# Strassen products of one stage: sums by vector adds, or accumulated in PSUM

## The chip, the cores and the metric

The kernel runs on one core of a Trainium2 chip. The metric is the device time of one execution in microseconds (us); less is better. Engine names are those of the profile: PE (TensorE), DVE (VectorE), ACT (ScalarE), POOL (GpSimd), SP (SyncE, which only issues transfers here).

## The reference, cut to what matters

```python
attn_out = _attn_ref(q, k, v, phi)            # 4 x 8 x 576 x 64, over 32 memory rows
x = transposed(attn_out)                      # 2304 tokens x 512
x = (x @ w_a * (x @ w_b)) @ w_out             # first block, d_ff 1536
h = x @ w_in                                  # second block, d_ff 2048
g = h * (1.0 / (1.0 + np.exp(-1.702 * h)))
out = g @ w_out2
```

The change touches only `h = x @ w_in` and the gate `g`. The second block's input, its last product and all before it stay as they are.

## The kernel before, in words

**Numbers in two parts.** Float32 products are made from two reduced-precision parts of each operand, hi and lo: hi·hi, lo·hi and hi·lo are added up (`PASSES`). `hi_lo` (line 308) makes them: ACT copies hi out, and then DVE or POOL subtracts hi from the source to get lo (`combine`, the instruction at line 305). The weights come as doubles and are decoded on the chip (lines 424 to 439).

**The stage.** `h = x @ w_in` is done in 24 groups (g, p): g counts eight strips of 256 hidden units, p three thirds of the tokens (2 x 384). A group is a 2 x 2 block product, made from seven products instead of eight, as Strassen and Winograd do. `PRODUCTS` pairs an operand of the weights (A11, A12, A22 and four combinations S1 to S4, all in the slot `win[g]`) with one of the tokens (B11, B21, B22, T1 to T4, in `yc[p]`). A product is six matmuls 128x384 (line 1142: two rows by three passes) into one PSUM bank of the eight in `bank_m`; what has to be summed across products is done behind them. The order of a group is P1, P6, P7, P5, P3, P4, P2 (`quad`).

**The sums.** `kept` (line 1177) copies P1 to SBUF on ACT. `added` (line 1184) makes every other sum on DVE: a PSUM bank plus an earlier sum in SBUF, into a fresh slot of `hb_s`. There are seven such adds a group, by the table `SUMS`. Four of the sums are results: c11, c12, c21, c22. `gate` (line 1194) passes each through the gated function on ACT, and SP's queue stores it to the DRAM buffer `g2d` (line 1196), from which the last product reads it back.

**What sets the order.** The program is emitted once, at build time, by a planner (`Order`). Streams with priorities ask for an engine, a time and perhaps a slot; the planner keeps a clock per engine and emits next what starts first by its own cost figures. On the chip each engine then runs its list strictly in that order and waits on semaphores. `main` (priority 50) issues the PE work. Sums, copies and gates are spawned at priority 0, and the operands' splits and combinations have streams of their own: `combine_weights` fills `win[g]` once a slot is free, and `combine_tokens` fills `yc[p]`.

**The order of groups.** (0, 0) runs alone, ahead of the last eight products of the first block (`proj`, line 864). The rest follows in the order (1,0), (0,1), (1,1), (0,2), (1,2), then three p for each of g = 2 to 5, then (6,0), (6,1), (7,0), (7,1), (6,2), (7,2). `win_s` has two slots; the one of g is released by the last product of its third group, here P2. So the slot of g = 0 goes to g = 2 when (0, 2) ends, one group before (2, 0) needs it. After the stage come the last products (lines 1343 and 1374).

```python
if name == "P2" and p == NP - 1:
    win_s.release(win[g], t)
if name == "P1":
    od.spawn(0, kept(t, q, ps, "s"))
for other, out_, place in SUMS[name]:
    od.spawn(0, added(t, q, ps, other, out_, place, left))
```

Of the kernel before, what the change touches and what calls it, by code (L numbers as in the profile page):

```python
# [11 lines left out]
AF = mybir.ActivationFunctionType  # L12
ALU = mybir.AluOpType
# [6 lines left out]
PE, ACT, DVE, POOL = "PE", "ACT", "DVE", "POOL"  # L20
# [26 lines left out]
class Lengths:  # L47
    dve, act, psum = 68, 94, 52
# [128 lines left out]
def tile_mem_attention_moe_moe2(  # L177
# [13 lines left out]
    nc = tc.nc  # L191
# [7 lines left out]
    P = 128  # L199
# [16 lines left out]
    NG2 = F2 // (G2 * P)  # L216
    N2 = 384
    NP = NT // (2 * N2)
# [8 lines left out]
    od = Order()  # L227
# [9 lines left out]
    g2d = dram.tile([F2, NT], F32, name="g2d")  # L237
# [3 lines left out]
    bank_m, bank_a = Slots(banks[:2]), Slots(banks[2:])  # L241
# [11 lines left out]
    attn_m = [p1.tile([P, 2 * NHG * HT], F32R, name=f"attn{i}") for i in range(2)]  # L253
# [472 lines left out]
    py, pz, pv, bdw, g1_t, g1_all, eff_y, big = None, None, None, [], {}, [], [], {}  # L726

    def give(slots_, views):
        slots_.free += [[x, now()] for x in views]

    def now():
        return od.clock[PE]
# [199 lines left out]
    win_s, hb_s, f_s, fw_s, sb_s, tb_s = Slots(), Slots(), Slots(), Slots(), Slots(), Slots()  # L932
    wo2_t, blocks = {}, []

    def views(m, n, count, o=0):
        return [m[:, o + i * n:o + (i + 1) * n] for i in range(count)]

    YN, WN = N2, 4 * P
    CN, FN, SN, BN = 2 * DM, K4 * NB, 2 * K4 * P, DM
# [9 lines left out]
    def spare():  # L949
        return next(x for x in (whl_a, big["whl_b"]) if x is not wt["o1", NG1 - 1][0])  # L950
# [69 lines left out]
    def room_chunks(*flat):  # L1020
        for x in flat:
            od.mark(now(), "room", "o2", len(wo2))
            wo2.append(x.rearrange("p (i f) -> p i f", i=2))

    def room_split(*flat):
        give(sb_s, [x.rearrange("p (i c t) -> p i c t", i=2, c=K4) for x in flat])
# [101 lines left out]

    sums = {}

    def step(q, name):
        g, p = q
        a, b = PRODUCTS[name]
        t = yield "mark", "win", g, a
        for r in range(2):
            t = max(t, (yield "mark", "yc", p, r, b))
        t, ps = yield PE, t, 1040, bank_m
        w, y = win[g][0][a], yc[p][b]
        n = 0
        for r in range(2):  # L1140
            for (sw, mv) in PASSES:
                nc.tensor.matmul(ps[0][:, :N2], w[:, sw, r, :], y[mv][r], start=(n == 0), stop=(n == 5))  # L1142
                n += 1
        if name == "P2" and p == NP - 1:
            win_s.release(win[g], t)
        if name == "P1":
            od.spawn(0, kept(t, q, ps, "s"))
        left = [len(SUMS[name])]
        for other, out_, place in SUMS[name]:
            od.spawn(0, added(t, q, ps, other, out_, place, left))  # L1150

    SUMS = {
# [3 lines left out]
    }  # L1156
    USES = {"s": 2, "u2": 2, "u3": 2, "u4": 1}

    def get(q, name):
        t = yield "mark", name, q  # L1160
        return t, sums[q, name][0]

    def drop(q, name, t):
        x = sums[q, name]
        x[1] -= 1
        if x[1] == 0:
            hb_s.release(x[0], t)

    def put(t, q, name, s, place):
        sums[q, name] = [s, USES.get(name, 1)]  # L1170
        od.mark(t, name, q)
        if place:
            yield from gate(t, q, *place, s)

    def kept(t, q, ps, name):
        t, s = yield ACT, t, act(N2, True), hb_s
        nc.scalar.activation(out=s[0], in_=ps[0][:, :N2], func=AF.Copy)
        bank_m.release(ps, t)
        yield from put(t, q, name, s, None)

    def added(t, q, ps, other, name, place, left):
        t1, x = yield from get(q, other)
        t, s = yield DVE, max(t, t1), dve(N2), hb_s
        nc.vector.tensor_tensor(out=s[0], in0=ps[0][:, :N2], in1=x[0], op=ALU.add)  # L1184
        left[0] -= 1
        if left[0] == 0:
            bank_m.release(ps, t)
        drop(q, other, t)
        yield from put(t, q, name, s, place)

    def gate(t, q, j, u, c):
        g, p = q
        t, _ = yield ACT, t, act(N2)
        nc.scalar.activation(out=c[0], in_=c[0], func=AF.Gelu_apprx_sigmoid)  # L1194
        k, o = G2 * g + j, (2 * p + u) * N2
        nc.sync.dma_start(out=g2d[k * P:(k + 1) * P, o:o + N2], in_=c[0])
        hb_s.release(c, t + 2500.0)
        od.mark(t, "g2", q, j, u)

# [38 lines left out]
    def split_gated():  # L1238
        for i, o in QUARTERS:
            t = yield "mark", "f", i, o  # L1240
            slot, f = loaded.pop(("f", i, o))
            for s in range(2):
                yield from split_part(t, f[:, :, s * P:(s + 1) * P], "sb", i, o, s)
            for s in range(2):
                t = max(t, (yield "mark", "sb", i, o, s))
            f_s.release(slot, t)
        od.mark(t, "front")
        for i in range(NQ, NW):
            yield from (split_whole(i) if i < NS else sums_gated(i))
# [178 lines left out]
    order = [(0, 0), (1, 0), (0, 1), (1, 1), (0, 2), (1, 2)]  # L1428
# [12 lines left out]
    def main():  # L1441
# [67 lines left out]
        yield from gated(g, 3, 1)  # L1509
        room_gated()  # L1510
        yield from quad(0, 0)
        yield from proj(g, 3, 0)
        yield from proj(g, 3, 1)
# [2 lines left out]
        room_projected()  # L1516
        od.spawn(6, load_gated())
        od.spawn(5, split_gated())
        for q in order[1:]:
            yield from quad(*q)  # L1520
            if q == (NG2 - 1, 0):
                room_chunks(*views(big["wv"], CN, 6), *views(spare(), CN, 2), *views(big["y0"], CN, 2, 14 * WN))
            if q == (NG2 - 1, 1):
                room_split(*views(attn_m[0], SN, 4), *views(attn_m[1], SN, 2))
        od.spawn(9, room_last())
        yield from proj2([(i, s) for i in range(NF) for s in range(2)])
        for i in range(NF, NW):
            yield from (proj2([(i, 0), (i, 1)]) if i < NS else proj2_seven(i))

    def quad(g, p):  # L1530
        for name in ("P1", "P6", "P7", "P5", "P3", "P4", "P2"):
            yield from step((g, p), name)

    with tc.manual_schedule():

# [12 lines left out]
        for n in range(NU):  # L1548
            p = 10 + n if n >= NHG else 10 + PC * n
# [42 lines left out]
```

## Time and profile before

| | us |
|---|---|
| time, median of 3 runs (lowest, highest) | 767.47 (766.93, 768.99) |
| span of the profiled execution | 765.3 |
| PE busy | 752.5 (98%) |
| DVE busy | 613.2 (80%) |
| ACT busy | 386.0 (50%) |
| POOL busy | 359.4 (47%) |

The profile gives the profiled execution its span, from the first instruction to the last, and no other time; the 2.2 us between the span and the median lie outside what the engines show. The table's busy times are means over stages with different limits, so the views that cut the span into stretches say more: they show in which stretch an engine has idle time at all. In rows of the trace, `bank` is a PSUM bank, `wv`, `whl_a`, `attn`, `eff`, `g`, `rest` and `y` are SBUF regions that hold the operands of the stage, `dm` holds decoded weights, and `acc` is a large SBUF region in which the sums and the intermediate tokens lie. A line starts with the time from the start of the span and the duration.

### The profile page before, as it was taken

The page shows a single profiled execution, that of the slowest core. Times are in us where ns is not written, and L with a number is a line of the kernel's source. Part 1 is how long each engine was busy: PE and PEld are TensorE (multiplying, and loading weights), DVE is VectorE, ACT ScalarE, POOL GpSimd, SP SyncE. Part 2 cuts the span into 40 slices and gives each one's busy share as a digit, 9 for nine tenths or more (in the row PEclk, how much of TensorE's full clock was granted, in tenths as well). Part 3 has the DMA queues.
Part 4 walks back from the last instruction along what each step waited for, and adds up shares of the span by engine and source line. Part 5 has one row for each costly group of instructions (what it writes and reads, how often), then busy time and mean ns, then how long its engine had stood idle before and what let it go on. Part 6 is the DMA issues. An engine that isn't in the chain of part 4 may idle for free.

```text
span 765.3 us, 14870 instructions
## 1 busy us (share of the span) xinstructions
PE 752.5 (98%) x5538; PEld 692.7 (91%) x5538; DVE 613.2 (80%) x1086; ACT 386.0 (50%) x854; POOL 359.4 (47%) x335
## 2 busy tenths in 40 slices
PE   8998999999999999999999999999999999999997
PEld 7787788999888979989999999999998888899997
DVE  4888978888877896347999878778796898898884
ACT  4577767454344352225465555454554465444441
POOL 0223442444435342226798655433271059776661
PEclk9999999999999999999999999999999999999999
DMA  8968313232321331000023546454669957544401
GB/s 262 339 213 247 113 38 112 76 108 84 114 79 56 92 113 46 1 1 2 1 69 101 176 149 189 158 179 147 219 241 328 307 179 245 178 139 138 136 23 37
DMA packets 70568, 103.99 MB, mean 136 GB/s; under 512 B 6240, under 2 KB 49248, under 8 KB 70496
## 3 DMA queue, kind: packets, MB, share of 16 engines
q1 hardware_dynamic: 65040, 93.64, 38.4%
q10 hardware_dynamic: 5456, 9.41, 3.5%
q8 instruction: 43, 0.70, 0.4%
q14 instruction: 29, 0.24, 0.1%
HBM read 75.24 MB, written 27.79 MB: 135 GB/s over the span
## 4 chain that ended last, share of the span: by engine, by line
PE 91%; DMA 3%; SPq 2%; DVE 2%; ACT 1%; issue 1%; ACTq 0%; DVEq 0%
PE bank L1142 23%; PE bank L831 19%; PE bank L1374 13%; PE bank L1343 12%; PE bank L887 10%; PE bank L864 10%; PE bank L760 3%; DMA q<-in_q_dram 2%; SPq L320 1%; DMA phi<-in_phi_dram 1%; DMA raw<-in_moe_w_b_dram 1%; SPq L321 1%; PE bank L1436 1%; PE bank L582 1%; SPq L352 0%
## 5 line engine op out<-in xcount | busy, mean ns | idle before, releaser
L305 POOL TENSOR_TENSOR acc<-acc 128x512 f32<-128x512 f32 (+2 forms) x67 | 93.4, 1416 | 75.7 <-ACT attn L311 31.9
L305 DVE TENSOR_TENSOR attn<-acc,attn 128x512 fp32r<-128x512 f32 (+1 forms) x102 | 107.4, 1079 | 13.6 <-ACT attn L311 13.6
L1184 DVE TENSOR_TENSOR acc<-bank,acc 128x384 f32<-128x384 f32 x168 | 89.6, 553 | 30.3 <-PE bank L1142 19.8
L311 ACT ACTIVATE attn<-acc 128x512 fp32r<-128x512 f32 (+2 forms) x117 | 70.6, 611 | 52.5 <-PE bank L1374 31.8
L844 ACT ACTIVATE gr<-bank 128x288 f32<-128x288 f32 x96 | 38.9, 405 | 81.9 <-PE bank L831 67.0
L305 POOL TENSOR_TENSOR y<-gr,y 128x288 fp32r<-128x288 f32 x45 | 38.0, 845 | 78.7 <-ACT y L311 78.5
L1194 ACT ACTIVATE acc<-acc 128x384 f32<-128x384 f32 x96 | 49.1, 522 | 51.0 <-DVE acc L1184 50.0
L847 DVE TENSOR_TENSOR gr<-bank,gr 128x288 f32<-128x288 f32 x96 | 43.4, 454 | 36.2 <-PE bank L831 27.9
L831 PE MATMUL bank<-attn,eff 128*128 128x288 f32 x384 | 54.2, 296 | 0.0
L831 PEld LDWEIGHTS bank<-attn,eff 128*128 128x128 f32 x384 | 51.9, 188 | 1.9 <-ACT plain L424 0.8
L864 PEld LDWEIGHTS bank<-g,whl_b 128*128 128x128 f32 x384 | 51.4, 188 | 1.7 <-ACT g L311 1.7
L864 PE MATMUL bank<-g,whl_b 128*128 128x288 f32 x384 | 52.7, 296 | 0.0
L1142 PE MATMUL bank<-attn,y 128*128 128x384 f32 x288 | 52.3, 335 | 0.0
L907 DVE TENSOR_TENSOR acc<-bank,acc 128x512 f32<-128x512 f32 (+1 forms) x72 | 38.7, 554 | 16.4 <-PE bank L887 15.6
L887 PE MATMUL bank<-y,whl_a 128*128 128x512 f32 (+1 forms) x240 | 51.6, 370 | 0.0
L887 PEld LDWEIGHTS bank<-y,whl_a 128*128 128x128 f32 x240 | 41.4, 188 | 9.8 <-issue 0.8
L1142 PEld LDWEIGHTS bank<-attn,y 128*128 128x128 f32 x288 | 50.1, 188 | 0.0
L305 POOL TENSOR_TENSOR g<-gr,g 128x288 fp32r<-128x288 f32 x28 | 26.1, 937 | 34.9 <-ACT g L311 34.7
L1374 PE MATMUL bank<-y,attn 128*128 128x256 f32 x300 | 41.1, 280 | 0.0
L831 PE MATMUL bank<-attn,eff_b 128*128 128x288 f32 x288 | 40.0, 295 | 0.0
L831 PEld LDWEIGHTS bank<-attn,eff_b 128*128 128x128 f32 x288 | 38.9, 188 | 0.2
L1374 PEld LDWEIGHTS bank<-y,attn 128*128 128x128 f32 x300 | 38.0, 188 | 0.1
(289 smaller groups left out, 1854.9 us busy)
## 6 DMA issues: line engine op xcount, KB each, us to landing
g2d<-acc SPq DMA_DIRECT2D x96, 192.0 KB, 2.1
raw<-in_moe_w_out_dram SPq DMA_DIRECT2D x28, 512.0 KB, 4.4
acc<-g2d SPq DMA_DIRECT2D x10, 1024.0 KB, 6.8
raw<-in_moe_w_in_dram SPq DMA_DIRECT2D x16, 512.0 KB, 3.7
acc<-g2d SPq DMA_DIRECT2D x16, 512.0 KB, 5.8
raw<-in_moe_w_a_dram SPq DMA_DIRECT2D x20, 256.0 KB, 2.8
raw<-in_moe_w_b_dram SPq DMA_DIRECT2D x20, 256.0 KB, 3.1
q<-in_q_dram SPq DMA_DIRECT2D x32, 144.0 KB, 4.4
```

Of the source, the lines that this page charges most:

```text
L305: (nc.gpsimd if e == POOL else nc.vector).tensor_tensor(out=dst, in0=in0, in1=in1, op=op)
L311: nc.scalar.activation(out=hi, in_=src, func=AF.Copy)
L831: nc.tensor.matmul(ps[0][:, :U], e[c][:, sw, i * CW + j * P:i * CW + (j + 1) * P], attn(b, mv, c, u * U, U), start=(n == 0), stop=(n == 3 ...
L844: nc.scalar.activation(out=gr[0], in_=pa_[0][:, :U], func=AF.Copy)
L847: nc.vector.tensor_tensor(out=gr[0], in0=pb[0][:, :U], in1=gr[0], op=ALU.mult)
L864: nc.tensor.matmul(ps[0][:, :U], w[:, sw, j, mb * P:(mb + 1) * P], g1[0][:, j, mv, :], start=(n == 0), stop=(n == 3 * G1 - 1),)
L887: nc.tensor.matmul(ps[0][:, :e - o], w[:, sw, j, mb * P:(mb + 1) * P], g1_all[mv][:, j, o:e], start=(n == 0), stop=(n == 3 * G1 - 1),)
L1142: nc.tensor.matmul(ps[0][:, :N2], w[:, sw, r, :], y[mv][r], start=(n == 0), stop=(n == 5))
L1184: nc.vector.tensor_tensor(out=s[0], in0=ps[0][:, :N2], in1=x[0], op=ALU.add)
L1194: nc.scalar.activation(out=c[0], in_=c[0], func=AF.Gelu_apprx_sigmoid)
L1343: nc.tensor.matmul(ps[i, s][0], b[0][:, sw, c - o, :], wo2[c][:, mv], start=(c == n == 0), stop=(c == 4 * K4 - 1 and n == 2),)
L1374: nc.tensor.matmul(ps[name][0][:, :NB], x[0][:, sw, c, :], moving(b, h // 2 + c, mv), start=(h == c == n == 0), stop=(h > 0 and c == K4 - ...
```

## The change

**Sums in PSUM.** A group's order is now P1, P5, P6, P3, P7, P2, P4. P1, P6, P7 and P4 accumulate into one bank (chain a), P5 and P3 into a second (chain b), and P2 has a third (c). A chained product adds to what is in the bank. Between them ACT takes copies: s after P1, x5 after P5, u2 after P6. DVE makes three adds: c12 = bank b + u2 after P3, c22 = bank a + x5 after P7, c11 = bank c + s after P2, each in place of its SBUF operand. c21 is what stands in bank a after P4, and the gate reads it straight from PSUM (`direct`).

**Waits.** The first matmul of a chained product waits until the sum that stood in the bank has been taken (`AFTER`): P6 for the copy s, P3 for x5, P7 for u2, and P4 for DVE's add c22.

**Two groups alternate.** `quads` sorts the steps of all groups behind (0, 0): step i of the n-th has the key 7n + 2i. So the second half of a group alternates with the first half of the next. (0, 0) stays alone, its steps one behind the other.

**The slot's release** moves with the last step, from P2 to P4.

The matmuls and their operands are the same in number and size: 1008 of line 1142 (now line 1153). DVE's adds go from 168 to 72 (line 1180), ACT's copies from 24 to 72 (line 1172); the 96 gates and 96 stores stay, and 24 of the gates read PSUM.

```diff
+    CHAINS = {"P1": "a", "P6": "a", "P7": "a", "P4": "a", "P5": "b", "P3": "b", "P2": "c"}
+    AFTER = {"P6": "s", "P3": "x5", "P7": "u2", "P4": "c22"}
+    held = {}
...
-        t, ps = yield PE, t, 1040, bank_m
+        chain = CHAINS[name]
+        first = (q, chain) not in held
+        if first:
+            t, held[q, chain] = yield PE, t, 1040, bank_m
+        else:
+            t = max(t, (yield "mark", AFTER[name], q))
+            t, _ = yield PE, t, 1040
+        ps = held[q, chain]
...
-                nc.tensor.matmul(ps[0][:, :N2], w[:, sw, r, :], y[mv][r], start=(n == 0), stop=(n == 5))
+                nc.tensor.matmul(
+                    ps[0][:, :N2], w[:, sw, r, :], y[mv][r], start=(first and n == 0), stop=(n == 5),
+                    skip_group_check=not first,
+                )
...
-        if name == "P2" and p == NP - 1:
+        if name == STEPS[-1] and p == NP - 1:
             win_s.release(win[g], t)
...
+        if name in ("P1", "P5", "P6"):
+            od.spawn(0, kept(t, q, ps, {"P1": "s", "P5": "x5", "P6": "u2"}[name]))
+        elif name == "P4":
+            od.spawn(0, direct(t, q, ps))
+        else:
+            od.spawn(0, added(t, q, ps, *SUMS[name]))
...
+    STEPS = ("P1", "P5", "P6", "P3", "P7", "P2", "P4")
+    SUMS = {"P7": ("x5", "c22", (1, 1)), "P3": ("u2", "c12", (0, 1)), "P2": ("s", "c11", (0, 0))}
...
+    def added(t, q, ps, other, name, place):
+        t = max(t, (yield "mark", other, q))
+        x = sums.pop((q, other))
+        t, _ = yield DVE, t, dve(N2)
+        nc.vector.tensor_tensor(out=x[0], in0=ps[0][:, :N2], in1=x[0], op=ALU.add)
+        od.mark(t, name, q)
+        if name != "c22":
+            bank_m.release(ps, t)
+        yield from gate(t, q, *place, x[0], x, act(N2))
+
+    def direct(t, q, ps):
+        s = yield "slot", hb_s
+        t = yield from gate(max(t, s[1]), q, 1, 0, ps[0][:, :N2], s, act(N2, True))
         bank_m.release(ps, t)
...
+        nc.scalar.activation(out=s[0], in_=src, func=AF.Gelu_apprx_sigmoid)
...
+    def quads(which):
+
+        steps = [(len(STEPS) * n + 2 * i, q, name) for n, q in enumerate(which) for i, name in enumerate(STEPS)]
+        for _, q, name in sorted(steps, key=lambda x: x[0]):
+            yield from step(q, name)
```

**PE, group (0, 0).** Seven products before, by the order P1, P6, P7, P5, P3, P4, P2; `bank_N` are PSUM banks.

```order
-L1142 MATMUL bank_75<-wv,y_1443 128x384 x6
-L1142 MATMUL bank_72<-whl_a,y_1443 128x384 x6
-L1142 MATMUL bank_74<-whl_a,y_1443 128x384 x2
-L1142 MATMUL bank_74<-y_1443 128x384 x4
-L1142 MATMUL bank_73<-wv,y_1443 128x384 x6
-L1142 MATMUL bank_77<-wv,y_1443 128x384 x6
-L1142 MATMUL bank_76<-y_1443 128x384 x6
-L1142 MATMUL bank_78<-wv,y_1443 128x384 x6
```

And with the change, P1, P5, P6, P3, P7, P2, P4:

```order
+L1153 MATMUL bank_75<-wv,y_1443 128x384 x6
+L1153 MATMUL bank_72<-wv,y_1443 128x384 x6
+L1153 MATMUL bank_75<-whl_a,y_1443 128x384 x6
+L1153 MATMUL bank_72<-wv,y_1443 128x384 x6
+L1153 MATMUL bank_75<-whl_a,y_1443 128x384 x2
+L1153 MATMUL bank_75<-y_1443 128x384 x4
+L1153 MATMUL bank_74<-wv,y_1443 128x384 x6
+L1153 MATMUL bank_75<-y_1443 128x384 x6
```

Before, every product has its own bank. Now four of the seven go to bank_75, and the last of them follows the fifth with one product between.

**DVE beside that group, before.** `attn_92<-acc,attn_92` makes lo parts of the tokens' second third, line 426 decodes weights, line 1184 makes the sums.

```order
L305 TENSOR_TENSOR attn_92<-acc,attn_92 128x384 x2
L1184 TENSOR_TENSOR acc<-bank_72,acc 128x384 [waits PE_49,Activation_49,Pool_49]
L426 TENSOR_SCALAR acc<-acc 128x512 [waits Pool_49]
L1184 TENSOR_TENSOR acc<-bank_74,acc 128x384 [waits DVE_49,PE_49]
L1184 TENSOR_TENSOR acc<-bank_73,acc 128x384 [waits PE_49]
L1184 TENSOR_TENSOR acc<-bank_73,acc 128x384 [waits DVE_49]
L1184 TENSOR_TENSOR acc<-bank_77,acc 128x384 [waits DVE_49,PE_49]
L430 TENSOR_SCALAR acc<-acc 128x512
L1184 TENSOR_TENSOR acc<-bank_76,acc 128x384 [waits PE_49]
L434 SCALAR_TENSOR_TENSOR acc<-raw_79,acc 128x512 [waits DMAHW3_49,DVE_49]
L1184 TENSOR_TENSOR acc<-bank_78,acc 128x384 [waits PE_49]
```

With the change:

```order
L305 TENSOR_TENSOR attn_92<-acc,attn_92 128x384 x2
L305 TENSOR_TENSOR acc<-acc 128x384 [waits DVE_49]
L305 TENSOR_TENSOR attn_92<-acc,attn_92 128x384
L426 TENSOR_SCALAR acc<-acc 128x512 [waits Activation_49]
L1180 TENSOR_TENSOR acc<-bank_72,acc 128x384 [waits PE_49,Activation_49]
L305 TENSOR_TENSOR acc<-acc 128x384 [waits DVE_49]
L1180 TENSOR_TENSOR acc<-bank_75,acc 128x384 [waits PE_49]
L1180 TENSOR_TENSOR acc<-bank_74,acc 128x384 [waits PE_49]
```

Before, one sum stood between the lo parts and line 426. Now two more instructions on tokens (`acc<-acc` is a combination, `attn_92` a lo part) stand there, and a third between c12 (bank_72) and c22 (bank_75, for which P4 waits).

**PE where the slot of g = 0 goes to g = 2, with the change.** The first row ends P4 of (0, 2), which releases the slot; bank_75 is P3 of (1, 2), bank_74 is P1 of (2, 0), bank_78 is P7 of (1, 2).

```order
L1153 MATMUL bank_77<-y_1443 128x384
L1153 MATMUL bank_75<-eff_b,y_1443 128x384 [waits Activation_49]
L1153 MATMUL bank_75<-eff_b,y_1443 128x384 x5
L1153 MATMUL bank_74<-wv,y_1443 128x384 [waits Activation_49]
L1153 MATMUL bank_74<-wv,y_1443 128x384 [waits DVE_49]
L1153 MATMUL bank_74<-wv,y_1443 128x384 x4
L1153 MATMUL bank_78<-rest,y_1443 128x384 x6
L1153 MATMUL bank_73<-wv,y_1443 128x384 [waits Activation_49]
```

**DVE at the same place, before.** `y_1443<-dm_84` is the lo part of A11 of g = 2, `y_1443<-dm_85` that of A22.

```order
L1184 TENSOR_TENSOR acc<-bank_72,acc 128x384 [waits PE_49]
L1184 TENSOR_TENSOR acc<-bank_74,acc 128x384 [waits PE_49]
L305 TENSOR_TENSOR y_1443<-dm_84,y_1443 128x256 [waits Activation_49]
L1184 TENSOR_TENSOR acc<-bank_77,acc 128x384 [waits PE_49,Activation_49]
L305 TENSOR_TENSOR y_1443<-dm_85,y_1443 128x256 [waits Activation_49]
```

With the change:

```order
L1180 TENSOR_TENSOR acc<-bank_76,acc 128x384 [waits PE_49]
L1180 TENSOR_TENSOR acc<-bank_75,acc 128x384 [waits PE_49,Activation_49]
L305 TENSOR_TENSOR y_1443<-dm_84,y_1443 128x256 [waits Activation_49]
L305 TENSOR_TENSOR dm_85<-dm_84,dm_85 128x2x128 [waits Pool_49]
L305 TENSOR_TENSOR y_1443<-dm_85,y_1443 128x256 [waits Activation_49]
```

Before, the seven products of (1, 2) stood on PE between the release and P1 of (2, 0); now it is one product. P1 of (2, 0) waits for the lo part, which stands on DVE right behind the add that needs the end of P3 of (1, 2).

## Rows read from the trace of the kernel before

**Rows 1.** Busy time of each engine in five stretches; columns as the head says.

```profile
core 0: us, PE busy (x) PEld busy (x) DVE busy (x) ACT busy (x) POOL busy (x), PEclk, DMA share, GB/s
0.00:105.00 105.00, 96.44 (x1142) 81.00 (x1143) 84.31 (x197) 67.13 (x174) 31.51 (x33) 1.00 0.69 219
105.00:391.00 286.00, 285.95 (x2119) 258.35 (x2118) 222.80 (x422) 131.38 (x306) 125.28 (x126) 1.00 0.20 62
...
404.70:572.40 167.70, 167.70 (x968) 167.70 (x967) 134.97 (x242) 90.03 (x195) 88.77 (x88) 1.00 0.52 174
572.40:761.10 188.70, 188.70 (x1225) 171.97 (x1223) 157.58 (x207) 88.32 (x164) 100.71 (x78) 1.00 0.54 174
761.10:765.30 4.20, 0.00 (x0) 0.00 (x0) 0.42 (x1) 0.00 (x0) 0.00 (x0) 1.00 0.45 120
```

**Rows 2.** The chain that ended last: start us, us, what.

```profile
404.76 167.65 PE bank L1142 x966
```

**Rows 3.** Costliest groups: the page's; then by form, 391 to 573 us.

```profile
L1142 PE MATMUL bank<-attn,y 128*128 128x384 f32 x288 | 52.3, 335 | 0.0
...
L1184 DVE TENSOR_TENSOR acc<-bank,acc 128x384 f32<-128x384 f32 x167 | 89.1, 553 | 30.3 <-PE bank L1142 19.8 <-ACT dm L424 4.8 <-ACT y L311 1.6
...
L1194 ACT ACTIVATE acc<-acc 128x384 f32<-128x384 f32 x92 | 47.4, 523 | 51.0 <-DVE acc L1184 50.0
...
L1177 ACT ACTIVATE acc<-bank 128x384 f32<-128x384 f32 x24 | 11.7, 487 | 5.4 <-PE bank L1142 5.4
```

**Rows 4.** Timeline of PE, 390.9 to 405 us: products 1 and 7.

```profile
390.96 1.21 PE L1142 MATMUL bank<-wv,y 128*128 128x384 f32 x6
...
397.21 1.20 PE L1142 MATMUL bank<-wv,y 128*128 128x384 f32 x6
```

**Rows 5.** Timeline of DVE, 391 to 400 us.

```profile
392.21 2.09 DVE L305 TENSOR_TENSOR attn<-acc,attn 128x384 fp32r<-128x384 f32 x2
394.23 0.55 DVE L1184 TENSOR_TENSOR acc<-bank,acc 128x384 f32<-128x384 f32 x1
394.69 0.77 DVE L426 TENSOR_SCALAR acc<-acc 128x512 f32<-128x512 f32 x1
395.38 1.94 DVE L1184 TENSOR_TENSOR acc<-bank,acc 128x384 f32<-128x384 f32 x4
```

**Rows 6.** DVE's groups by form, 391 to 573 us: two SBUF inputs.

```profile
L305 DVE TENSOR_TENSOR attn<-acc,attn 128x384 fp32r<-128x384 f32 x4 | 4.5, 1132 | 0.0
...
L305 DVE TENSOR_TENSOR acc<-acc 128x384 f32<-128x384 f32 x3 | 3.1, 1021 | 0.0
...
L305 DVE TENSOR_TENSOR g<-acc,whl_b 128x384 fp32r<-128x384 f32 x1 | 0.5, 548 | 0.0
```

**Rows 7.** Timeline of POOL, 392 to 400 us.

```profile
393.85 1.33 POOL L305 TENSOR_TENSOR acc<-acc 128x384 f32<-128x384 f32 x1
395.14 1.19 POOL L305 TENSOR_TENSOR attn<-acc,attn 128x384 fp32r<-128x384 f32 x1
396.30 4.64 POOL L305 TENSOR_TENSOR acc<-acc 128x384 f32<-128x384 f32 x4
```

**Rows 8.** Timeline of ACT, 391 to 394 us: the copy of P1.

```profile
392.68 0.47 ACT L1177 ACTIVATE acc<-bank 128x384 f32<-128x384 f32 x1
```

**Rows 9.** Timelines of PE and of DVE around the hand-over of a weight slot.

```profile
432.71 0.51 PE L1142 MATMUL bank<-eff_b,y 128*128 128x384 f32 x2
...
441.05 1.20 PE L1142 MATMUL bank<-wv,y 128*128 128x384 f32 x6
...
433.95 0.56 DVE L1184 TENSOR_TENSOR acc<-bank,acc 128x384 f32<-128x384 f32 x1 [0.48 <-PE bank L1142]
434.68 0.75 DVE L305 TENSOR_TENSOR y<-dm,y 128x256 fp32r<-128x256 f32 x1 [0.17 <-ACT y L311]
...
436.58 0.55 DVE L305 TENSOR_TENSOR y<-dm,y 128x256 fp32r<-128x256 f32 x1
```

**Rows 10.** Timeline of DVE, 564 to 573 us, the last groups of products.

```profile
568.76 0.86 DVE L305 TENSOR_TENSOR wv<-dm,wv 128x512 fp32r<-128x512 f32 x1 [0.16 <-ACT wv L458]
```

More of the change, by code (lines that the diff above doesn't have):

```diff
@@ L1141, in step @@
             for (sw, mv) in PASSES:
-                nc.tensor.matmul(ps[0][:, :N2], w[:, sw, r, :], y[mv][r], start=(n == 0), stop=(n == 5))
+                nc.tensor.matmul(
+                    ps[0][:, :N2], w[:, sw, r, :], y[mv][r], start=(first and n == 0), stop=(n == 5),
+                    skip_group_check=not first,
+                )
                 n += 1
-        if name == "P2" and p == NP - 1:
+        if name == STEPS[-1] and p == NP - 1:
             win_s.release(win[g], t)
[L1146 to L1152, printed above, removed]
[3 rows of a table removed]
[L1156 to L1173, printed above, removed]
+        if name in ("P1", "P5", "P6"):
[6 more added lines that the diff above has]
+    SUMS = {"P7": ("x5", "c22", (1, 1)), "P3": ("u2", "c12", (0, 1)), "P2": ("s", "c11", (0, 0))}
     def kept(t, q, ps, name):
@@ L1177, in kept, with gate @@
         nc.scalar.activation(out=s[0], in_=ps[0][:, :N2], func=AF.Copy)
-        bank_m.release(ps, t)
[L1179 to L1191, printed above, removed]
+        sums[q, name] = s
+        od.mark(t, name, q)
[4 more added lines that the diff above has]
+        nc.vector.tensor_tensor(out=x[0], in0=ps[0][:, :N2], in1=x[0], op=ALU.add)
+        od.mark(t, name, q)
+        if name != "c22":
[4 more added lines that the diff above has]
+        t = yield from gate(max(t, s[1]), q, 1, 0, ps[0][:, :N2], s, act(N2, True))
+        bank_m.release(ps, t)
+    def gate(t, q, j, u, src, s, cost):
         g, p = q
-        t, _ = yield ACT, t, act(N2)
-        nc.scalar.activation(out=c[0], in_=c[0], func=AF.Gelu_apprx_sigmoid)
+        t, _ = yield ACT, t, cost
+        nc.scalar.activation(out=s[0], in_=src, func=AF.Gelu_apprx_sigmoid)
         k, o = G2 * g + j, (2 * p + u) * N2
-        nc.sync.dma_start(out=g2d[k * P:(k + 1) * P, o:o + N2], in_=c[0])
-        hb_s.release(c, t + 2500.0)
+        nc.sync.dma_start(out=g2d[k * P:(k + 1) * P, o:o + N2], in_=s[0])
+        hb_s.release(s, t + 2500.0)
         od.mark(t, "g2", q, j, u)
+        return t
     NF, NQ, NS, NW = 3, 4, 4, NT // NB
@@ L1518, in main @@
         od.spawn(5, split_gated())
[L1519 to L1524, printed above, removed]
+        yield from quads(order[1:])
         od.spawn(9, room_last())
@@ L1530, in quad @@
     def quad(g, p):
-        for name in ("P1", "P6", "P7", "P5", "P3", "P4", "P2"):
+        for name in STEPS:
             yield from step((g, p), name)
+    def quads(which):
+        steps = [(len(STEPS) * n + 2 * i, q, name) for n, q in enumerate(which) for i, name in enumerate(STEPS)]
+        for _, q, name in sorted(steps, key=lambda x: x[0]):
+            yield from step(q, name)
+            if name == STEPS[-1]:
+                if q == (NG2 - 1, 0):
+                    room_chunks(*views(big["wv"], CN, 6), *views(spare(), CN, 2), *views(big["y0"], CN, 2, 14 * WN))
+                if q == (NG2 - 1, 1):
+                    room_split(*views(attn_m[0], SN, 4), *views(attn_m[1], SN, 2))
     with tc.manual_schedule():
```

3 rows, old and new, of the table SUMS are left out of this document.

## The prediction

> **What bounds the kernel now.** I read the busy time of each engine by stretch first. In [rows 1] PE has idle time only before 105 us and in the last 4.2 us: it is busy for 285.95 of 286 us after that, for all of 167.70 us in the stage of the change, and for all of 188.70 us behind it. In the same stage DVE works 134.97 us, ACT 90.03 and POOL 88.77, so all three have room. The granted clock is 1.00, the level of 2.4 GHz, in every stretch. The chain of waits says the same thing in another way: [rows 2] is one line of 966 matmuls without a wait between them, 167.65 / 966 = 0.1735 us each. The PE timeline of group (0, 0) agrees: seven products in a row, six steps in 397.21 - 390.96 = 6.25 us [rows 4], 1.04 us per product. So the stage lasts as long as its matmuls, and nothing that another engine saves can shorten it. Only two things can move the time: fewer or denser matmuls on PE, or a new wait of PE.
>
> **What the change takes away.** 168 - 72 = 96 adds of DVE at 0.553 us [rows 3], 53 us. It hides no PE wait, since there is none: worth 0. DVE's list gets shorter, which helps only what waits for DVE, in the parts below. PE's matmuls stay 1008, at the same spacing: 0. Gates and stores stay at 96: 0.
>
> **What it adds and hides.** 48 copies on ACT at 0.487 us [rows 3], 23 us. ACT goes from 90 to some 113 us in a stage of 168 us. A gate that reads PSUM where it read SBUF has no row; the nearest are the copy from PSUM, 0.487, and the gate from SBUF, 0.523 [rows 3], and on an engine with 55 us free either is 0.
>
> **What it adds on PE: waits.** Before, a product got a bank of its own and PE waited for no sum. Now the first matmul of P6, P3, P7 and P4 waits until a copy or an add has emptied the sum out of its bank, and PE runs in order, so everything behind it waits too. In the alternating groups three other products stand between the product whose sum is taken and the one that waits, 3 x 1.04 = 3.1 us for a copy of 0.49 us with some 0.04 us of hand-over on each side. That is cover for 2.5 us of other work ahead of the copy on ACT or of the add on DVE: four or five instructions. I take 0 there, and rival D prices it. The cover is thin in three places, which I found from the order of the instructions.
>
> *Group (0, 0), alone.* Here only one product stands between. The copies are short enough: s is made at 392.68 + 0.47 = 393.15 us [rows 8], and P6, the third product, is due at 390.96 + 2 x 1.04 = 393.04, a tenth late at most. The add c22 is another matter. P4 is the seventh product, due at 397.21 us [rows 4]. On DVE c22 stands behind the two lo parts after which the next instruction begins at 394.23 us [rows 5], then a combination, a lo part, line 426, c12 and another combination. The combinations have 1.02 us and the lo part 1.13 us in this stage [rows 6], line 426 takes 0.69 to the next start and an add 0.46 [rows 5]: 394.23 + 1.02 + 1.13 + 0.69 + 0.46 + 1.02 + 0.55 = 399.1 us. DVE starts the next instruction about 0.08 us before the end of one (0.55 against 0.46), three times 0.08 comes off, 398.9 us. P4 waits **1.7 us**. The low end: with POOL idle such an instruction takes 0.548 us [rows 6], 0.47 to the next, and c22 ends at 394.23 + 3 x 0.47 + 0.69 + 0.46 + 0.55 = 397.34, a wait of 0.2 us with the hand-over. The high end: each of the three waits for one whole POOL instruction, 4.64 / 4 = 1.16 us [rows 7], before its own 0.55, which gives 394.23 + 3 x 1.63 + 0.69 + 0.46 + 0.55 = 400.8, a wait of 3.6 us. I take the middle one, because POOL is busy without a break here [rows 7] and the lo parts just before took 2.09 us for two [rows 5].
>
> The Trainium skill has a rule for this on its page "SBUF — State Buffer", section "Who interferes with whom": a VectorE instruction with two SBUF inputs and a GpSimd instruction that reads SBUF want the same read port, whoever is first keeps it for the whole instruction, and the other stands still. The trace agrees that the two disturb each other (1132 ns beside POOL, 548 ns in the quickest row [rows 6]), but a mean of 1132 is less than a whole POOL instruction and its own 548 would make. By the rule at its hardest the sum would be 1.9 us larger than by the rows.
>
> *The hand-over of the slot of g = 0 to g = 2.* Before, the slot was free after 433.06 us or a little later, when the matmuls of P2 of (0, 2) that begin at 432.71 were through, and P1 of (2, 0) began at 441.05 [rows 9], a whole group later. Now P4 of (0, 2) releases it and one product, P3 of (1, 2), stands between. Say P3 begins at 0. Its last matmul begins at 0.87 and ends 0.335 later [rows 3], at 1.20. DVE's add of its sum comes next in DVE's list and the lo part of A11 behind it. The add begins at 1.24, the lo part 0.46 later at 1.70, and it takes 0.55 to 0.75 us [rows 9]: 2.25 to 2.45. P1's second matmul, which needs it, is due at 1.04 + 0.17 = 1.21. PE waits **1.1 us** (0.9 to 1.4). It can't be nothing, because the lo part can't run ahead of an add that needs P3's end. Later slots have eight products or more.
>
> *The end of the stage.* The last group has nothing to alternate with. Its P4 waits for c22, and ahead of c22 on DVE stands a lo part of the next weights, of 0.86 us, that itself waits for ACT [rows 10]. With one product of 1.04 us between, an add of 0.55 fits and 0.86 + 0.55 does not: **0.3 us** (0 to 1.0, the low end if DVE has done it before P7 ends).
>
> The rest goes together: two more instructions than before in the SBUF slots of the sums, and three loads of the gated values that stand six stores earlier on SP's queue. They have no wait of PE to lengthen, since PE's operands there were ready early in every product of the stage [rows 2]: 0.
>
> **The sum.** 1.7 + 1.1 + 0.3 = 3.1 us. The profiled execution has a span of 765.3 us, which would become 768.4; the median of the runs is 2.2 us above that span, and 767.47 + 3.1 = **770.6 us**. Ends: 0.2 + 0.9 + 0 = 1.1, 768.6 us, and 3.6 + 1.4 + 1.0 = 6.0, 773.5 us.
>
> **Rivals.**
>
> *B, not slower.* DVE's instructions on tokens at (0, 0) run without POOL's interference, because with the shorter list they meet POOL at other times. Then c22 is ready at 397.3, the first wait is 0.2, and 0.2 + 1.1 + 0.3 = 1.6 gives 769.1 us, no difference that can be told. It decides from the point at which the three instructions take less than 2.1 us together, 0.7 each, where the first wait falls to 0.9. For it: the quickest row is 0.548 [rows 6]. Against it: POOL's unbroken work [rows 7]. DVE also gets to these instructions earlier or later by the sums it no longer makes, which I can't see.
>
> *C, DVE stands still for whole POOL instructions.* The first wait is 3.6, the total 5.0, 772.5 us. For it: the slowest means of [rows 6]. Against it: at 1132 they are well under 1.16 + 0.55 = 1.71. The Trainium skill's rule above would have it so.
>
> *D, PE waits in the steady part too.* ACT and DVE run in order, and a copy behind a decode that waits for its transfer is late: DVE's sums waited 4.8 us in all behind such decodes of ACT [rows 3]. At 0.2 to 0.4 us for each of 23 groups it adds 5 to 9 us to the 3.1: 775 to 780. Against it: 2.5 us of cover at every step.
>
> *E, faster.* PE would need denser matmuls; [rows 2] leaves no idle time to win in the stage. Below 765.2 us.
>
> **How the numbers follow.** A change of 0.3%, 2.3 us, is about what a measurement of this kernel can tell from none: 765.2 to 769.8 us counts as the same. Chances: the forecast 0.55, B 0.25, C 0.08, D 0.08, E 0.04. Of the forecast's 0.55 some 0.08 lies under 769.8, between its end of 768.6 and the bound. So the same has 0.25 + 0.08 = 0.33, slower 0.47 + 0.08 + 0.08 = 0.63, faster 0.04. The forecast's own range is 768.6 to 773.5. Reaching to B with all three waits at their low ends, and half a us below for the scatter of the runs shown (766.93 against 767.47), needs 768.0; D, E and the edges of B are left out. The whole range is 768.0 to 773.5 us.
>
> **What would show it.** In the profile of the changed kernel PE should have idle time in the stage of some 3 us: 1.7 us ahead of P4 of (0, 0), released by DVE's add of line 1180, near 397 us; 1.1 us after the first matmul of P1 of (2, 0), released by line 305 of DVE; and a few tenths in the last group. DVE's busy time should fall by some 50 us and ACT's rise by some 23, with PE's the same. The forecast is wrong if the idle time is spread over the groups (D), if the wait at (0, 0) is under 0.9 us (B) or over 3 (C), or if the spacing of the matmuls differs from 0.1735 us.

## The result and the profile after

The changed kernel takes 773.15 us (772.36 to 774.02, 4 runs), beside 768.23 us (766.93 to 769.07, 4 runs) for the kernel before: a ratio of 1.0075, 95% interval 1.0062 to 1.0089. It is slower, by some 5 to 6 us where 3.1 were forecast. The profiled execution's span is 770.6 us, 5.3 more than before. All of that lies in the stage of the change: from its first matmul to the first of the next stage PE takes 186.63 us instead of 181.29, and what follows takes as long as it did.

First, the busy time of each engine in five stretches of the changed kernel, as in [rows 1]: length, then busy time of PE, PEld, DVE, ACT and POOL, then the granted clock, the DMA share and GB/s.

```profile
105.00:391.00 286.00, 285.95 (x2119) 258.35 (x2118) 222.71 (x422) 130.79 (x306) 126.02 (x126) 1.00 0.19 62
391.00:404.70 13.70, 12.36 (x78) 11.73 (x78) 12.60 (x19) 9.97 (x20) 12.55 (x12) 1.00 0.16 57
404.70:574.00 169.30, 168.07 (x968) 167.17 (x968) 101.35 (x166) 106.65 (x239) 65.59 (x67) 1.00 0.49 163
574.00:577.00 3.00, 2.06 (x12) 1.74 (x11) 2.45 (x4) 1.55 (x4) 2.76 (x2) 1.00 0.99 331
577.00:766.00 189.00, 189.00 (x1227) 172.46 (x1226) 158.82 (x206) 87.56 (x163) 100.36 (x78) 1.00 0.55 177
```

PE is still busy for 285.95 of 286 us ahead of the stage and for all of the 189 us behind it, and the granted clock is 1.00 throughout. It is idle in rows two to four. The chain of waits, which was one line of 966 matmuls in [rows 2], says where:

```profile
398.48 0.48 DVE acc L1180
399.01 1.31 PE bank L1153 x6
...
406.66 32.32 PE bank L1153 x186
...
440.68 0.91 DVE y L305
441.63 124.14 PE bank L1153 x713
...
575.82 0.56 DVE acc L1180
576.42 1.32 PE bank L1153 x6
```

The chain leaves PE in three places and no more: ahead of the P4 of (0, 0), ahead of P1 of (2, 0), and ahead of the last P4. These are the three places of the forecast. Between them PE runs 186 and 713 matmuls without a break, so the alternating groups do cover their waits.

The PE timeline gives the sizes, as the distance between the starts of neighbouring matmuls over the 173.3 ns that is usual:

| place | forecast us | measured us | of it |
|---|---|---|---|
| (0, 0) | 1.7 | 1.88 | P6 0.15, P4 1.51, restarts 0.22 |
| slot for g = 2 | 1.1 | 1.72 | first matmul of P1 0.31, second 1.30, restart 0.11 |
| last group | 0.3 | 1.54 | P7 0.22, P4 1.10, restarts 0.22 |
| spacing elsewhere | 0 | 0.21 | 997 matmuls, more than the like distances of the kernel before |
| sum | 3.1 | 5.35 | stage 186.63 - 181.29 = 5.34 |

"Restart" is a cost that the forecast didn't have. The matmul behind the one that waited begins 281 to 284 ns later, not 173: some 0.11 us more, five times in this stage.

### The profile page after: what moved, and what is told of

It is laid out like the page before. It is cut to its first block, busy times and chain, and to the rows that moved or that the text cites. A ratio compares the mean times of both kernels' runs of the same rounds, so it can differ in the third digit from the quotient of the medians.

```text
span 770.6 us, 14785 instructions
## 1 busy us (share of the span) xinstructions
PE 755.0 (98%) x5538; PEld 693.5 (90%) x5538; DVE 582.7 (76%) x1011; ACT 404.1 (52%) x902; POOL 338.8 (44%) x314
## 4 chain that ended last, share of the span: by engine, by line
PE 88%; DVE 4%; DMA 3%; SPq 2%; ACT 1%; issue 1%; ACTq 0%; DVEq 0%
PE bank L1153 21%; PE bank L831 18%; PE bank L1375 13%; PE bank L1344 12%; PE bank L887 10%; PE bank L864 10%; PE bank L760 3%; DMA q<-in_q_dram 2%; SPq L352 1%; PE bank L501 1%; DMA raw<-in_moe_w_out_dram 1%; DMA raw<-in_moe_w_b_dram 1%; SPq L321 1%; PE bank L582 0%; DVE dm L434 0%
## 5 line engine op out<-in xcount | busy, mean ns | idle before, releaser
L305 DVE TENSOR_TENSOR attn<-acc,attn 128x512 fp32r<-128x512 f32 (+1 forms) x104 | 109.3, 1080 | 15.6 <-ACT attn L311 15.4
L305 POOL TENSOR_TENSOR acc<-acc 128x512 f32<-128x512 f32 (+2 forms) x63 | 90.9, 1466 | 37.4 <-DVE attn L305 25.2
L1180 DVE TENSOR_TENSOR acc<-bank,acc 128x384 f32<-128x384 f32 x72 | 39.8, 554 | 57.4 <-PE bank L1153 41.7
L1194 ACT ACTIVATE acc<-acc 128x384 f32<-128x384 f32 x72 | 37.4, 522 | 38.7 <-DVE acc L1180 38.7
L1153 PE MATMUL bank<-attn,y 128*128 128x384 f32 x288 | 56.8, 335 | 0.0
L305 POOL TENSOR_TENSOR y<-acc,y 128x256 fp32r<-128x256 f32 (+1 forms) x21 | 18.8, 911 | 69.6 <-ACT y L311 69.6
L1172 ACT ACTIVATE acc<-bank 128x384 f32<-128x384 f32 x72 | 35.0, 486 | 12.7 <-PE bank L1153 11.1
```

The costliest lines, as they stand in the source:

```text
L305: (nc.gpsimd if e == POOL else nc.vector).tensor_tensor(out=dst, in0=in0, in1=in1, op=op)
L1180: nc.vector.tensor_tensor(out=x[0], in0=ps[0][:, :N2], in1=x[0], op=ALU.add)
```

## The experiments

The first 105 us vary from execution to execution by up to 3.8 us, in instructions that all these kernels share (in one run the granted clock was 0.70 between 30 and 40 us). So the stage's length is compared, from the first matmul of the stage to the first of the next. It is that of one profiled execution of each kernel; the ratio beside it is over all executions of the kernel.

| kernel | stage us | against before | ratio, 95% interval |
|---|---|---|---|
| before | 181.29 | | |
| changed | 186.63 | +5.34 | 1.0075, 1.0062 to 1.0089 |
| P4 of (0, 0) behind four projection products | 185.44 | +4.15 | 1.0081, 1.0063 to 1.0100 |
| (2, 0) moved back | 186.52 | +5.23 | 1.0124, 1.0109 to 1.0139 |
| last group alternates | 185.12 | +3.83 | 1.0059, 1.0044 to 1.0074 |
| these three | 184.20 | +2.91 | 1.0047, 1.0030 to 1.0064 |
| old sums, alternating | 186.50 | +5.21 | 1.0061, 1.0041 to 1.0080 |
| chains, not alternating | 188.42 | +7.13 | 1.0100, 1.0084 to 1.0115 |
| first and third edit, (0, 2) and (1, 2) drawn forward | 181.88 | +0.59 | 1.0017, 1.0006 to 1.0029 |
| lo parts behind c22 | 185.73 | +4.44 | one execution, no interval |

**P4 of (0, 0) behind four products of the projection.**

```diff
-        yield from quad(0, 0)
-        yield from proj(g, 3, 0)
+        for name in STEPS[:-1]:
+            yield from step((0, 0), name)
+        yield from proj(g, 3, 0)
+        yield from step((0, 0), STEPS[-1])
```

> Group (0, 0)'s last product P4 moves behind four products of the first block's projection; nothing else differs from the changed kernel. Theory (three places where PE waits, 1.9 + 1.7 + 1.5 us): the wait of 1.5 us for c22 goes, with the 0.1 us that the matmul behind a wait loses; the 0.3 us ahead of P6 of (0, 0) stay. Span 770.6 - 1.6 = 769.0. Rival (what PE waits for is late anyway, and a removed wait comes back at the next one): span stays at 770.6 and PE waits longer in the projection or in the next groups.

The wait is gone, as the PE timeline of this run shows: P4 (the second row) runs right behind the four projection products (the first).

```profile
397.98 3.33 PE L864 MATMUL bank<-g,whl_b 128*128 128x288 f32 x24
401.14 1.21 PE L1153 MATMUL bank<-y 128*128 128x384 f32 x6
```

The 1.6 us are won there, but the stage gains 1.19, because a new wait stands at 463.7 us: 0.3 us for a copy of ACT and 0.1 of restart. So the rival has a small part of it. The ratio, on an interval of 0.4%, can't tell this kernel from the changed one. The place is what is shown, by the trace.

**(2, 0) moved back by a few steps.**

```diff
+            if q == (2, 0):
+                return k + (4, 5.5, 6, 8, 10, 12, 13.5)[i]
+            return k + 2 * i
```

> The products of (2, 0) move back so that three products of (1, 2), not one, stand between the release of the weight slot and P1 of (2, 0). Theory: the 1.7 us at the hand-over go (0.4 ahead of the first matmul, 1.3 ahead of the second and third), span 768.9; its own spacings of two products cost nothing, since copies of 0.5 us need only one product of cover when ACT is free. Rival (a removed wait comes back): P5, P6 or P3 of (2, 0), or P4 of (1, 2), wait for about as long, span 770.6.

This is a miss for my theory. P1 no longer waits, but the third product of (2, 0), P6, does, for its hi part and then for its lo part. The PE timeline of this run:

```profile
446.62 1.21 PE L1153 MATMUL bank<-wv,y 128*128 128x384 f32 x6
449.37 0.44 PE L1153 MATMUL bank<-whl_a,y 128*128 128x384 f32 x1 [1.54 <-ACT y L311]
450.71 1.14 PE L1153 MATMUL bank<-whl_a,y 128*128 128x384 f32 x5 [0.90 <-DVE y L305]
```

P6 needs a combination of the weights that is made behind several others. The last matmul of P4 of (0, 2), which frees the slot, begins at 441.24 and takes 0.33; P6's first begins at 449.37, 7.8 us after the release. The slot of g = 1 becomes free some 5 us after that of g = 0, and ACT's hi parts of another strip (`y<-acc`, where those of g = 2 are `y<-dm`) come between; in the changed kernel they don't. How much of the 7.8 us is theirs was not tried by itself. So the hand-over isn't one lo part behind one add. It is seven operands: in the changed kernel the last lo part of the seven ends 7.6 us after the release, and here P6's own ends after 9.1. The forecast priced the first of the seven.

The stage's length hides two things. The slot costs 2.98 us in this run, 1.26 more than in the changed kernel. And the last group, which this edit doesn't touch, costs 0.11 us where it was 1.54: the planner has emitted the lists of DVE and ACT anew, c22 begins as soon as P7 is through, at 578.2 us, and P4 doesn't wait, with one product between as before. So what stands ahead of c22 decides that wait, not the one product of cover.

The ratio is above what the stage shows. In the profiled execution 2.6 us of the difference lie ahead of the stage and 0.6 behind it, where PE waits once for line 305 of DVE. The other executions of this kernel had a lower granted clock still, 0.992 to 0.996 over the span against 0.998 in the profiled one; where they lost it isn't on record.

**The last group alternates with the one before it to the end.**

```diff
+            if q == (NG2 - 1, 2):
+                return k - 6 + 2 * i
+            return k + 2 * i
```

> The last group (7, 2) starts six steps earlier, so that it alternates with (6, 2) to the end and its P4 has three other products between itself and P7. Theory: the 1.5 us in the last group go (0.3 ahead of P7, 1.2 ahead of P4), span 769.1. Rival (what PE waits for here is the load and decode of the last stage's weights, for which ACT and DVE are late): the last stage's first product waits in its place, span 770.6 or little less.

As the theory had it: the stage loses 1.5 us, the waits at (0, 0) and at the slot stay as they were, and none is left behind 443.3 us. All of PE's waits in the stage, in total us, number and longest:

```profile
PE bank L1153 <- DVE acc L1180: 1.3, 1, 1.3
PE bank L1153 <- DVE y L305: 1.0, 1, 1.0
```

The next stage begins without a wait and takes as long as it did, so the rival falls.

**These three edits at once.**

> All three edits at once. Theory: the three waits add up and are all of the difference, so 770.6 - 1.6 - 1.7 - 1.5 = 765.8 us of span, some 0.5 above the kernel before (765.3): 0.3 ahead of P6 of (0, 0) and 0.2 from the spacing of matmuls. Time against before 1.0005, within 0.2%. Rival (a removed wait comes back, or the stage itself is slower): 768 to 771, ratio 1.004 or more.

This is the rival's outcome: the ratio is 1.0047, the span of 767.9 us stands at the rival's lower edge, and a removed wait has come back. (0, 0) keeps its 0.3 and the last group nothing, but the slot costs 2.45 us. The waits of PE in this run:

```profile
PE bank L1153 <- ACT y L311: 1.5, 1, 1.5
PE bank L1153 <- POOL y L305: 0.4, 1, 0.4
```

It is P6 of (2, 0) again, with 1.5 us for its hi part and 0.4 for its lo part. (This table counts from the end of the matmul before; by the distances between starts it is 1.71 and 0.63, with 0.11 of restart.) As the second edit alone already emptied the last group, this run doesn't tell what the third adds to it.

**(0, 2) and (1, 2) drawn forward, in place of moving (2, 0) back.**

```diff
-            if q == (2, 0):
-                return k + (4, 5.5, 6, 8, 10, 12, 13.5)[i]
+            if q == (0, 2):
+                return k + (0, 2, 4, 5.5, 6, 6.5, 8)[i]
+            if q == (1, 2):
+                return k + (0, 2, 3, 4, 5, 6, 8)[i]
```

> As the kernel with all three edits, but the hand-over is mended from the other side: (2, 0) stays where the change puts it, and (0, 2) is finished earlier and (1, 2) drawn together, so that five products stand between the release of the slot and P1 of (2, 0) and eight between the release and P6 of (2, 0). Theory (an operand of P6 needs about 8 us from the release, by the run in which (2, 0) was moved back and P6 waited in place of P1): the last wait of 1.7 to 2.5 us goes; stage 181.3 + 0.3 ahead of P6 of (0, 0) + 0.2 of spacing = 181.8, up to 182.3 if the drawn-together (1, 2) waits once. Ratio to before 1.000 to 1.001. Rival (something else delays the operands): stage 183.5 or more, as with all three edits.

The stage is 181.88 us; 181.8 was expected. No wait is left behind (0, 0) but for 0.14 us at 441.7. The chain of this run has the whole stretch behind (0, 0) in one line again, 167.97 us for 966 matmuls where [rows 2] has 167.65:

```profile
394.56 6.53 PE bank L1153 x36
408.48 167.97 PE bank L1153 x966
576.45 88.69 PE bank L1344 x384
```

So the three places are all of the difference but 0.6 us, of which 0.27 is P6 of (0, 0), 0.14 the wait just named and the rest spacing. The chained sums win nothing either: the ratio is 1.0017 (1.0006 to 1.0029), and no version here beats the kernel before.

**The old sums, alternating.** (The kernel before with `quads` for the groups behind (0, 0).)

> The kernel before, with its seven adds a group and a bank for every product, but groups behind (0, 0) alternate as in the change; the slot is released behind P2, its last step. Theory (three separate places): no wait at (0, 0) and none in the last group, since no product waits for a sum; only the slot's hand-over is left, one product between release and P1 of (2, 0), and PE waits there 1.5 to 3 us. Stage 181.3 + 1.5 to 3 = 182.8 to 184.3 us. Rival (chains in PSUM are what costs, alternating is free): stage 181.3.

The rival falls: alternating alone costs 5.21 us. 2.3 of them are the slot, within what the theory gave. Two parts were not foreseen. (0, 2) needs the last third of the tokens earlier, and DVE, with seven adds a group, has a lo part of it late by 0.96 us, with the restart 1.07 (the first row of the timeline below). And right behind the slot's waits PE ran at half its clock. The windows (columns as above) and the PE timeline of this run:

```profile
441.00:444.70 3.70, 1.92 (x10) 1.34 (x9) 1.74 (x3) 3.23 (x8) 2.75 (x4) 1.00 0.29 106
444.70:448.20 3.50, 3.50 (x13) 3.50 (x12) 1.97 (x4) 1.28 (x4) 1.63 (x2) 0.51 0.01 2
```

```profile
426.77 0.79 PE L1142 MATMUL bank<-g,y 128*128 128x384 f32 x3 [0.80 <-DVE g L305]
...
443.58 1.14 PE L1142 MATMUL bank<-whl_a,y 128*128 128x384 f32 x5 [0.92 <-POOL y L305]
...
445.35 0.84 PE L1142 MATMUL bank<-eff,y 128*128 128x384 f32 x2
```

The granted clock is 0.51 there, and ten matmuls stand some 320 ns apart instead of 173: 1.6 us. In the changed kernel's stage the clock stays at 1.00. The wait at (0, 2) points to how the two halves of the change fit together: with DVE's 96 adds still there, the alternating order has its tokens late, and in the changed kernel it doesn't. That DVE's load is what decides it was not tried by itself.

**Chains, not alternating.**

```diff
-        steps = [(len(STEPS) * n + 2 * i, q, name) for n, q in enumerate(which) for i, name in enumerate(STEPS)]
+        steps = [(len(STEPS) * n + i, q, name) for n, q in enumerate(which) for i, name in enumerate(STEPS)]
```

> The changed kernel without alternating groups: every group's seven products one behind the other, so that one product (1.04 us) stands between a sum and the product that waits for it, everywhere. Theory: the slot's hand-over costs nothing, (0, 0) and the last group cost the same 1.9 and 1.5 us, and in the 22 groups between a copy or an add comes late whenever ACT or DVE has over 0.45 us of other work ahead of it: of 4 waits a group perhaps 1 or 2 are late, by 0.4 us and 0.1 us of restart each, 10 to 25 us in all. Stage 181.3 + 13 to 28 = 195 to 210 us. Rival (one product of cover is enough): stage under 187 us.

Nearer to the rival: 188.42 us. Of the 7.1 us, 1.9 are (0, 0) and 0.9 the last group. The rest is 4.1 us in ten places. Three of them make 2.9: 1.0 us for a copy of ACT at 420.6, 0.6 and 1.3 us for adds of DVE at 563.0 and 571.5. The other seven are waits of up to 0.15 us, each with 0.11 of restart. So in most groups one product of 1.04 us is almost enough cover for a copy of 0.49 or an add of 0.55, and I had priced the other work ahead of it too high. Alternating is worth 1.8 us against this, net of the slot's 1.7.

**The lo parts behind c22.** Those of chunks 1 to 3 of the last stage's weights are made only when c22 of the last group is; PE's order stays.

```diff
+            if c in (1, 2, 3):
+                t = max(t, (yield "mark", "c22", (NG2 - 1, 2)))
             t2 = yield from combine(t, wo2[c][:, LO], m[0], f32(wo2[c][:, HI]), ALU.subtract, DM)
```

> The changed kernel, order of PE as it is, but the lo parts of the last stage's weight chunks 1, 2 and 3 are not made before the add c22 of the last group. Theory (P4 of the last group waits because DVE has that lo part ahead of c22, and the lo part waits for ACT): the wait of 1.1 us ahead of P4 goes and the 0.2 us ahead of P7 stays; the lo parts, 1.3 us each on POOL or DVE, are then late for the first products of the last stage, and PE waits there 1 to 2 us. Span 770 to 772. Rival (one product of cover is too little for c22 whatever stands on DVE): P4 still waits 0.5 us or more.

Between the two. DVE's and PE's timelines of this run:

```profile
573.31 1.67 DVE L439 SCALAR_TENSOR_TENSOR dm<-raw,dm 128x512 uint32<-128x512 uint32 x1
574.91 1.01 DVE L1182 TENSOR_TENSOR acc<-bank,acc 128x384 f32<-128x384 f32 x2
```

```profile
575.98 0.62 PE L1155 MATMUL bank<-rest,y 128*128 128x384 f32 x2 [0.33 <-DVE acc L1182]
```

P4's wait falls from 1.10 to 0.49 us, and P7's 0.22, which was expected to stay, is gone. What is left has another cause of the same kind: a decode step of 1.67 us now stands on DVE ahead of c12 and c22. As that step came in the lo part's place, the run doesn't tell exactly how much of the 1.10 was the lo part's. The rest of the kernel takes 0.9 us longer than in the changed kernel (189.76 against 188.87 from its first matmul to the end of its last): some 0.3 at 579.6 and 0.6 behind line 305 of DVE at 668.3. In this one execution that takes the gain back; whether the edit is the cause isn't shown.

## Why the prediction was right or wrong, step by step

The direction was right and the time lies in the range, but the change is nearly twice what was forecast: 5.3 us in the profiled execution against 3.1. The mechanism held, and two terms of the sum were mis-sized: the slot and the last group, whose 1.72 and 1.54 us lie above even their own high ends of 1.4 and 1.0. The time lies in the range by luck, in the room that the range had for a dearer (0, 0).

**Right: nothing to win.** PE was full in the stage, and 53 us of adds off DVE won nothing, as [rows 1, 2] had it. It was also right in saying what replaces them: waits of PE, in three places that the order of the instructions shows, and none in the steady part. Rival D is out, since PE runs 713 matmuls in one piece. Rival E is out as well.

**(0, 0): right, in part by luck.** 1.7 forecast, 1.62 measured for P4 and its restart, and 1.88 with P6, for which a tenth was named and left out of the sum. DVE's timeline of the changed kernel, to be held against [rows 5]:

```profile
394.20 1.37 DVE L305 TENSOR_TENSOR acc<-acc 128x384 f32<-128x384 f32 x1
395.49 0.55 DVE L305 TENSOR_TENSOR attn<-acc,attn 128x384 fp32r<-128x384 f32 x1
395.96 1.24 DVE L426 TENSOR_SCALAR acc<-acc 128x512 f32<-128x512 f32 x1
397.12 0.55 DVE L1180 TENSOR_TENSOR acc<-bank,acc 128x384 f32<-128x384 f32 x1
397.59 0.90 DVE L305 TENSOR_TENSOR acc<-acc 128x384 f32<-128x384 f32 x1
398.41 1.01 DVE L1180 TENSOR_TENSOR acc<-bank,acc 128x384 f32<-128x384 f32 x2
```

The three two-input instructions took 1.37, 0.55 and 0.90 us: 2.8 together, where the forecast had 3.17 by [rows 6] and rival B needed under 2.1. (With the overlap of starts and ends that the forecast took off elsewhere, 2.1 us would give a wait of 0.6 and not 0.9; B is out by either.) The step was right by two errors that cancel: line 426 took 1.24 instead of 0.69.

Rival C's price, a whole POOL instruction and 0.55 us each, 3 x 1.71, isn't what happened. POOL's timeline at the same place:

```profile
393.82 1.33 POOL L305 TENSOR_TENSOR attn<-acc,attn 128x384 fp32r<-128x384 f32 x1
395.65 1.27 POOL L305 TENSOR_TENSOR acc<-acc 128x384 f32<-128x384 f32 x1 [0.49 <-DVE acc L305]
396.87 1.20 POOL L305 TENSOR_TENSOR attn<-acc,attn 128x384 fp32r<-128x384 f32 x1
```

DVE's first and third two-input instruction began while one of POOL's ran, and ended 0.42 us behind its end, both; the second began ahead of POOL's and took 0.55. In the whole trace of the changed kernel 22 of DVE's instructions of line 305 on 128x384 began while one of POOL's ran: 20 of them ended 0.41 to 0.42 us behind its end, whatever was left of it. The three others took 0.55. So DVE waits for all that is left of POOL's instruction, and the forecast's argument against this, that the mean of 1132 ns is less than a whole POOL instruction and 548 would make, misses that POOL's instruction is partly over by then. The Trainium skill's page "SBUF — State Buffer", section "Who interferes with whom", says that the loser blocks fully until the other's instruction is done. The trace agrees, with the 0.41 to 0.42 us above. The same section of the Trainium skill says that a VectorE instruction with at most one SBUF input, outside its two-port modes, does not contend. The adds with one input in PSUM bear that out: they take 0.54 to 0.56 us here whatever POOL does. The same section of the Trainium skill says that `tensor_scalar` can contend. Line 426 at 395.96 fits: it ended 0.28 us behind POOL's instruction and took 1.24 us, where it takes 0.41 to 0.43 with POOL idle.

**The slot: the term was too small,** 1.1 for 1.72. The step that failed is the lo part's price of 0.55 to 0.75 us. PE, DVE, ACT and POOL at that place in the changed kernel:

```profile
440.16 0.44 PE L1153 MATMUL bank<-wv,y 128*128 128x384 f32 x1
441.63 1.14 PE L1153 MATMUL bank<-wv,y 128*128 128x384 f32 x5 [1.03 <-DVE y L305]
```

```profile
440.12 0.56 DVE L1180 TENSOR_TENSOR acc<-bank,acc 128x384 f32<-128x384 f32 x1 [2.64 <-ACT y L311]
440.60 0.98 DVE L305 TENSOR_TENSOR y<-dm,y 128x256 fp32r<-128x256 f32 x1
```

```profile
439.01 0.49 ACT L1194 ACTIVATE acc<-bank 128x384 f32<-128x384 f32 x1 [0.50 <-PE bank L1153]
439.39 1.02 ACT L311 ACTIVATE y<-dm 128x256 fp32r<-128x256 f32 x3
```

```profile
439.88 1.42 POOL L305 TENSOR_TENSOR y<-dm,y 128x256 fp32r<-128x256 f32 x2 [15.65 <-ACT y L311]
```

The lo part took 0.98 us, more than the dearest row of [rows 9]. It began 0.03 us behind the second of POOL's two instructions and ended 0.28 us behind its end. That is 0.33 us more than the middle of the forecast's price. The rest of the 0.6 is the restart, 0.11, and some 0.07 each for an add that began later than forecast and for hand-overs. The hi part was late as well, since on ACT the gate of c21, which the change made ready at just that moment, runs ahead of the three hi parts. So the first matmul of P1 waits 0.31 us; but the second waits for the lo part in any case, so that the 0.31 adds nothing to the sum of the two. The runs with (2, 0) moved back add what the forecast did not see at all: behind the first lo part come the other operands. In the changed kernel P6 of (2, 0) begins at 445.74, 6.8 us after the release, and 1.7 of these are P1's own waits, so mending P1 alone brings P6 too early. A third slot for the weights, which would take the hand-over away, was not tried.

**The last group: the step that failed most,** 0.3 for 1.54. The forecast took the lo part of [rows 10] at 0.86 us and set it against one product of cover. In the changed kernel, on ACT and on DVE:

```profile
572.59 0.48 ACT L1172 ACTIVATE acc<-bank 128x384 f32<-128x384 f32 x1
572.96 0.49 ACT L1194 ACTIVATE acc<-bank 128x384 f32<-128x384 f32 x1
573.33 1.16 ACT L458 ACTIVATE wv<-dm 128x512 fp32r<-128x512 f32 x2
```

```profile
573.60 0.55 DVE L1180 TENSOR_TENSOR acc<-bank,acc 128x384 f32<-128x384 f32 x1
574.52 1.38 DVE L305 TENSOR_TENSOR wv<-dm,wv 128x512 fp32r<-128x512 f32 x1 [0.38 <-ACT wv L458]
575.82 1.01 DVE L1180 TENSOR_TENSOR acc<-bank,acc 128x384 f32<-128x384 f32 x2
```

DVE stands idle from 574.14 to 574.52, waiting for ACT's second hi part, which stands behind a gate and the first. Then the lo part takes 1.38 us: POOL makes another lo part from 574.05 to 575.35, and DVE's ends 0.55 us behind that. So c22, whose sum is in the bank by 574.5, begins at 575.82. The forecast named the wait for ACT and gave it no price, and it took the duration from one row where [rows 6] had dearer ones. By the lo part alone the term is 0.52 us short. The chain of waits goes further back: it leaves PE at 565.8 us and comes back by two decode steps on DVE, of 1.70 us each, a gate and hi parts on ACT, and this lo part. P7's 0.2 us, behind the copy in the first row of ACT, which is late, was in no term. That what stands ahead of c22 decides P4's wait, the run with (2, 0) moved back shows, where the wait is gone.

**Restart and spacing: left out,** 0.55 and 0.2 us. There was no waiting matmul behind 105 us in the trace of before that would have shown the 0.11.

**DVE's busy time** fell by 30.5 us and not by some 50: 613.2 to 582.7 on the page. The planner gave DVE 21 instructions that POOL had done (POOL: 335 to 314 instructions, 359.4 to 338.8 us): 16 of line 305, on two SBUF inputs, and 5 of line 426. It filled DVE's free time with work, and the longest wait of each of the three places is for DVE. ACT's rose by 18 us where 23 were forecast.

## What to carry to other kernels

A saving on an engine that the bound one never waits for is worth nothing, and a chain in an accumulator buys it with waits that did not exist. Where the groups alternate, as here, the cost is not spread over the loop: it sits where the loop begins, ends and hands a buffer over, so these places are to be looked at one by one in the order of the instructions, with the whole queue ahead of the awaited instruction on its engine priced, the engine it waits for in turn included. An instruction of DVE on two SBUF inputs costs what is left of POOL's instruction at its start, and here 0.3 to 0.55 us more. A release that moves later is priced by the last operand that depends on it, not by the first.

## What the runs showed of the hardware that was not expected

A PE that has waited loses more than the wait: the next matmul begins 277 to 285 ns behind the one that waited, where 173 ns is usual, in nearly every wait of every run in the stage. Each small wait so costs 0.11 us on top.

What DVE loses to POOL on two SBUF inputs is regular in every run: an instruction of line 305 that begins while one of POOL's runs ends a fixed time behind POOL's, in the changed kernel 0.28 us for most of those on 128x256, 0.41 to 0.42 on 128x384 and 0.55 on 128x512, where it takes 0.41, 0.55 and 0.68 to 0.69 by itself.

PE's clock fell to 1.2 GHz within the stage in one run alone: granted 0.51 for 3.5 us, behind 3.7 us in which PE had been busy for 1.92. In the run with (2, 0) moved back PE was busy for 1.27 of 3.71 us at the like place, and the clock stayed at 1.00. Two runs that don't agree leave open what decides it.
